# A fused attention and soft-mixture kernel: fewer key columns in the loads, one small input carried in another's rows, and the first output columns stored in pairs of tiles

## The chip, the cores and the metric

The kernel runs on one core of a Trainium2 chip, as one launch. The metric is the device time of an execution in microseconds, the median of three runs. The times in the profile and in the rows below are microseconds from the start of the span of one profiled execution, if not marked ns.

## What is computed

Two blocks follow each other. The first is chunked attention: 4 batches x 8 heads, 768 tokens, head size 64. A chunk of 32 queries sees 8 memory keys, 16 tokens to its left, its own 32 and 8 to its right. The second is a soft mixture of 8 experts with 4 slots each; its input `x` is the attention's output as 3072 rows of 512.

```python
for c in range(24):                       # chunks of 32 tokens, per batch and head
    k_full = concat(mem_k, k[max(0, 32*c - 16) : min(768, 32*c + 40)])
    a = softmax(q[chunk c] @ k_full.T / 8);  out[chunk c] = a @ v_full
x = out as (3072, 512)
logits = x @ phi                          # phi: 512 x 32 slots
d = softmax over the rows of logits;  slot_input = d.T @ x          # 32 x 512
slot_out = relu(slot_input[e] @ w1[e]) @ w2[e]   # w1[e]: 512 x 1024, w2[e]: 1024 x 512
return softmax over the slots of logits @ slot_out
```

## The kernel before

Everything is float32, and every instruction is kept in the order in which the program writes it (`InOrder`, lines 52 to 64), so each engine's queue is what the text below says. All transfers are issued by SP, in one queue over 16 DMA engines, and a transfer uses all 16.

**Attention.** The 3072 rows are cut into 12 units of 256 (three to a batch; lines 20 to 36). Unit U needs queries (512 KB, `load_qk`, line 214), keys (two transfers, for even and odd heads, `load_k`, line 198) and values (768 KB, `load_v`, line 219). A unit's keys stand as a stream of 312 columns for each of four head pairs: memory keys, then two chunks, and so on, with 16 columns ahead and 8 behind. Where the unit before in the same batch holds the first 24 columns already (units 2, 4, 5, 7, 8, 10 and 11, `has_head`, line 67), only 288 are loaded and POOL copies the 24 over (`head_from_last`, `head_from_own`, lines 203 to 212). In a batch's first unit the first 16 columns, and in its last unit the last 8, are zeros that belong to no token; their scores are overwritten with -1e30 before the softmax (lines 265 to 267). Values come in three slabs of 512 columns; POOL builds a fourth slab and moves rows (`place_v`, line 223, five copies).

The loop at line 456 runs over the units as a pipeline: normalize unit U-1, transpose its output and unit U's weights, scores and softmax of U+1, values of U; then SP gets the loads of U+3 and a share of the weights (`load_w`). After every second unit 512 rows go through the logits and the dispatch sums (lines 327 to 419). `phi` is read first in `part_logits` (line 327), in unit 2; its load is issued once, at line 451, behind the values of unit 2.

**Experts.** Weights are kept in slabs of 128 x 1024, in places that come free one after the other (lines 140 to 154), mostly loaded two slabs to a transfer of 1 MB with rows of 8 KB. `w1` is used in `expert_in` (line 614), `w2` in `expert_out` (line 663). The output's 512 columns are worked in two halves (`NBLK` = 2, 256 columns each): for a half, eight experts are summed in one accumulation, the sum is copied (`slot_copy`, line 674), summed over its four groups by a matmul and copied again (`slot_rows`, line 677). Then six tiles of 512 rows (`combine`, line 689) each take four matmuls, copies by DVE and ACT into a free slab (`stage`, line 687) and a store of 512 KB with rows of 4 KB (line 710).

The order at the end is written out by hand (lines 713 to 727). While TensorE works the second half's experts 1 to 5, the first half's tiles 0 to 4 are combined, one behind each expert; the sixth comes behind the second half's sums, and then the six tiles of the second half:

```python
    shls, among = [None] * NBLK, (1, 2, 3, 4, 5)
    ...
    late = [(0, G) for G in range(len(among), NG)] + [(1, G) for G in range(NG)]
    for i, (blk, G) in enumerate(late):
        combine(blk, G, shls[blk], i % 2 == 1)
        if i == 0:
            shls[1] = slot_rows(1)
```

With the last argument true, `combine` takes four single PSUM banks and DVE makes two copies; with false it takes a pair of banks, and DVE makes one wide copy. Tile names in the rows: `s` scores, `a` values' sums, `kh` the copied key columns, `so` the experts' sums, `r` the sum over groups, `D` its copy for the second half, `o` a tile's matmuls.

## Time and profile before

| | |
|---|---|
| median of 3 runs | 160.84 us (160.62 to 160.93) |
| profiled execution | 159.95 us, of which the span is 158.2 us |
| TensorE, DVE, ACT, POOL busy | 141.4, 98.9, 74.4, 58.8 us |
| moved by DMA | 63.34 MB, 12457 packets, mean 400 GB/s |
| read from and written to HBM | 56.67 and 6.29 MB |

In the profile a group's line gives engine, operation, what it writes and reads, and how often; a transfer's landing is counted from its issue by SP until all 16 DMA engines have reported. The DMA share is the mean over the 16 engines; packets overlap a little, so that it can stand above 1.

### The profile page before, as it was taken

The page shows a single profiled execution, that of the slowest core. Times are in us where ns is not written, and L with a number is a line of the kernel's source. Part 1 is how long each engine was busy: PE and PEld are TensorE (multiplying, and loading weights), DVE is VectorE, ACT ScalarE, POOL GpSimd, SP SyncE. Part 2 cuts the span into 40 slices and gives each one's busy share as a digit, 9 for nine tenths or more (in the row PEclk, how much of TensorE's full clock was granted, in tenths as well). Part 3 has the DMA queues.
Part 4 walks back from the last instruction along what each step waited for, and adds up shares of the span by engine and source line. Part 5 has one row for each costly group of instructions (what it writes and reads, how often), then busy time and mean ns, then how long its engine had stood idle before and what let it go on. Part 6 is the DMA issues. An engine that isn't in the chain of part 4 may idle for free.

```text
span 158.2 us, 5938 instructions
## 1 busy us (share of the span) xinstructions
PE 141.4 (89%) x2577; PEld 99.5 (63%) x2577; DVE 98.9 (63%) x195; ACT 74.4 (47%) x165; POOL 58.8 (37%) x87
## 2 busy tenths in 40 slices
PE   7998789999999697999997998999999999998900
PEld 3457669786878594868785867656655555444500
DVE  7098969889787777698889489644552101334810
ACT  3032484866659466676585658140232200334710
POOL 8329858766083947655519450400000000000000
PEclk9999999999999999999999999999999999999995
DMA  5999999999999999999999999999999999999995
GB/s 158 327 410 420 408 420 423 421 412 428 410 431 410 421 421 423 415 429 410 423 419 424 433 419 421 419 402 339 407 425 421 431 421 427 414 418 369 374 410 207
DMA packets 12457, 63.34 MB, mean 400 GB/s; under 512 B 1552, under 2 KB 1680, under 8 KB 8848
## 3 DMA queue, kind: packets, MB, share of 16 engines
q1 hardware_dynamic: 12432, 62.97, 97.5%
q8 instruction: 20, 0.33, 0.8%
q14 instruction: 5, 0.04, 0.1%
HBM read 56.67 MB, written 6.29 MB: 398 GB/s over the span
## 4 chain that ended last, share of the span: by engine, by line
PE 79%; DVE 7%; issue 4%; DMA 3%; ACT 3%; POOL 1%; DVEq 0%; POOLq 0%
PE a L62 14%; PE s L62 12%; PE so L62 9%; PE h L62 9%; PE pt_ps L62 7%; PE xt_ps L62 6%; PE o L62 5%; PE D_ps L62 4%; PE lp L62 3%; DMA k<-in_kT_dram 3%; PE l L62 2%; DVE pt L62 2%; PE fill L62 2%; PE ht_ps L62 2%; DVE z L62 1%
## 5 line engine op out<-in xcount | busy, mean ns | idle before, releaser
L62 POOL COPY v<-v 32x512 f32<-32x512 f32 (+1 forms) x60 | 46.8, 780 | 29.0 <-DMA v<-in_vw_dram 25.5
L62 PEld LDWEIGHTS a<-v,pt 128*64 128x64 f32 x768 | 24.3, 138 | 13.8 <-ACT pt L62 6.6
L62 PE MATMUL a<-v,pt 128*64 128x64 f32 x768 | 27.0, 225 | 4.1 <-issue 2.5
L62 ACT COPY pt<-pt_ps 64x512 f32<-64x512 f32 (+1 forms) x48 | 26.1, 544 | 0.9
L62 PE MATMUL s<-k,q 128*32 128x128 f32 x712 | 24.4, 275 | 0.5 <-issue 0.3
L62 ACT ACTIVATE p<-p 128x512 f32<-128x512 f32 x24 | 15.1, 631 | 16.6 <-DVE p L62 16.2
L62 PEld LDWEIGHTS s<-k,q 128*32 128x32 f32 x712 | 20.7, 110 | 3.4 <-issue 3.3
L62 DVE TENSOR_REDUCE mx<-s 128x8 f32<-128x512 f32 x24 | 16.5, 688 | 6.5 <-PE s L62 6.2
L62 ACT COPY xT<-xt_ps 128x512 f32<-128x512 f32 x22 | 12.8, 586 | 12.6 <-PE xt_ps L62 12.5
L62 DVE TENSOR_TENSOR p<-s,mx 128x512 f32<-128x512 f32 x24 | 16.6, 692 | 0.8
L62 PE MATMUL pt_ps<-ident,p 128*128 128x128 f32 x96 | 15.0, 279 | 1.3 <-issue 1.1
L62 DVE TENSOR_TENSOR x<-a,z 128x512 f32<-128x512 f32 x22 | 14.7, 682 | 1.4 <-PE a L62 1.4
L62 DVE TENSOR_REDUCE z<-p 128x16 f32<-128x1040 f32 (+1 forms) x13 | 14.9, 1143 | 0.0
L62 PE MATMUL xt_ps<-ident,x 128*128 128x128 f32 x88 | 13.1, 273 | 0.6 <-DVE x L62 0.6
L62 PEld LDWEIGHTS pt_ps<-ident,p 128*128 128x128 f32 x96 | 10.7, 141 | 4.0 <-issue 2.8
L62 PE MATMUL h<-w,siT 128*32 128x256 f32 x208 | 12.1, 381 | 0.0
L62 PE MATMUL so<-w,pt 128*32 128x256 f32 x176 | 10.9, 382 | 0.0
L62 PEld LDWEIGHTS xt_ps<-ident,x 128*128 128x128 f32 x88 | 10.1, 141 | 0.9 <-DVE x L62 0.8
L62 PE MATMUL fill<-lp 128*128 128x512 f32 x12 | 8.5, 849 | 1.1 <-DVE lp L62 1.1
L62 PEld LDWEIGHTS h<-w,siT 128*32 128x32 f32 x208 | 6.4, 110 | 4.2 <-issue 0.3
L62 PEld LDWEIGHTS so<-w,pt 128*32 128x32 f32 x176 | 5.1, 109 | 4.7 <-issue 2.0
L62 ACT ACTIVATE xT<-h,rzd 128x512 f32<-128x512 f32 x4 | 2.8, 688 | 11.1 <-PE h L62 11.1
(119 smaller groups left out, 159.0 us busy)
## 6 DMA issues: line engine op xcount, KB each, us to landing
w<-in_w_dram SPq DMA_DIRECT2D x23, 1024.0 KB, 11.4
v<-in_vw_dram SPq DMA_DIRECT2D x12, 768.0 KB, 9.8
q<-in_qT_dram SPq DMA_DIRECT2D x12, 512.0 KB, 8.5
k<-in_kT_dram SPq DMA_DIRECT2D x14, 288.0 KB, 8.8
k<-in_kT_dram SPq DMA_DIRECT2D x10, 312.0 KB, 8.5
k<-in_w_dram SPq DMA_DIRECT2D x2, 1024.0 KB, 12.7
v<-in_w_dram SPq DMA_DIRECT2D x2, 1024.0 KB, 13.4
out_dram<-w SPq DMA_DIRECT2D x4, 512.0 KB, 6.4
```

Of the source, the lines that this page charges most:

```text
L62: return self.tc.keep_in_program_order(f(*args, **kwargs))
```

## The change

There are three edits.

Keys: a batch's first unit no longer loads the 16 columns of no token and a batch's last unit no longer loads its 8 (`k_cut`). The first unit's rows land 16 columns further on in the buffer, and the score matmul of the chunk at the edge reads what stands beside them, old but finite numbers; their scores are overwritten as before.

phi: the array `phi` is gone as an input of its own; its 64 KB stand behind the values of unit 1 in the same rows, `load_v(1)` brings them into the fourth slab's place, and POOL copies them out before it builds that slab.

Stores: tiles 0 and 1, 2 and 3, 4 and 5 of the first half are stored by one transfer each, 1 MB with rows of 8 KB, when the second of the two is copied. The sixth tile moves behind expert 6 of the second half, so that the second half's sums are followed at once by `slot_rows(1)` and its six tiles. These are stored one by one, as before.

```diff
+def k_cut(U):
+    t = U % UPB
+    return (LEFT if t == 0 else HALO if has_head(U) else 0), (RIGHT if t == UPB - 1 else 0)
...
-    def k_shift(U):
-        return HALO if has_head(U) else 0
+    def k_row(U):
+        lo, hi = k_cut(U)
+        return (LEFT if U % UPB == 0 else 0), KW - lo - hi
...
     def load_k(U, pars=range(2)):
-        n = NPAIR * (KW - k_shift(U))
+        at, n = k_row(U)
         for par in pars:
-            sp.dma_start(k_buf[U % 2][par:P:2, par, 0:n], kT[U, par, :, 0:n])
+            sp.dma_start(k_buf[U % 2][par:P:2, par, at:at + NPAIR * n], kT[U, par, :, 0:NPAIR * n])
...
     def load_v(U):
         if U < NU:
-            sp.dma_start(v_buf[U % NV][:, 0:3, :], vw[U].rearrange("p (s n) -> p s n", n=DM))
+            n = 3 * DM + (NKC * NSLOT if U == 1 else 0)
+            sp.dma_start(v_buf[U % NV].rearrange("p s n -> p (s n)")[:, 0:n], vw[U, :, 0:n])
...
         v = v_buf[U % NV]
+        if U == 1:
+            pool.tensor_copy(out=phi_sb.rearrange("p c s -> p (c s)"), in_=v[:, 3, 0:NKC * NSLOT])
...
-    sp.dma_start(phi_sb.rearrange("p c s -> p (c s)"), phi)
...
+    out_pair = out[0].rearrange("g p u n -> (g p u n)").rearrange("(h p m) -> h p m", h=NG // 2, p=P)
...
+    def store(blk, G):
+        if blk:
+            sp.dma_start(out[blk, G], stage[NG * blk + G])
+        elif G % 2:
+            f, o = places[order[G - 1]]
+            sp.dma_start(out_pair[G // 2], f[:, o:o + 2 * PIECE])
...
-        sp.dma_start(out[blk, G], o_sb)
+        store(blk, G)
...
-    shls, among = [None] * NBLK, (1, 2, 3, 4, 5)
+    shls, among = [None] * NBLK, (1, 2, 3, 4, 5, 6)
...
-    late = [(0, G) for G in range(len(among), NG)] + [(1, G) for G in range(NG)]
-    for i, (blk, G) in enumerate(late):
-        combine(blk, G, shls[blk], i % 2 == 1)
-        if i == 0:
-            shls[1] = slot_rows(1)
+    shls[1] = slot_rows(1)
+    for G in range(NG):
+        combine(1, G, shls[1], G % 2 == 1)
```

The rows of all values in HBM become 512 B longer, of which only unit 1's carry anything and only unit 1's are loaded in full. The host puts the paired rows of the first half back in order.

## Rows read from the trace of the kernel before

**Rows 1.** The page: busy tenths of the DMA engines in 40 equal slices of the span, the rate in each slice, and the share of the DMA engines' time that SP's queue took.
```profile
DMA  5999999999999999999999999999999999999995
GB/s 158 327 410 420 408 420 423 421 412 428 410 431 410 421 421 423 415 429 410 423 419 424 433 419 421 419 402 339 407 425 421 431 421 427 414 418 369 374 410 207
q1 hardware_dynamic: 12432, 62.97, 97.5%
```

**Rows 2.** Four transfers by themselves: the last weight load, the first store, the first store of the second half, the last store. Of the first and the last the issue on SP (start, duration); those of the other two stand in rows 3. Behind each issue its time to landing; the landings are in the order of the four.
```profile
125.21 0.33 SPq L62 DMA_DIRECT2D w<-in_w_dram  x1
...
DMA to landing us min/median/max: 17.0/17.0/17.0
...
DMA to landing us min/median/max: 7.0/7.0/7.0
...
DMA to landing us min/median/max: 3.5/3.5/3.5
...
151.74 1.15 SPq L62 DMA_DIRECT2D out_dram<-q  x1
...
DMA to landing us min/median/max: 5.5/5.5/5.5
```

**Rows 3.** Instructions in order of time: start, time from the first start to the last end of the group, engine and what it is. First around the first store, then around the end of the experts.
```profile
135.01 0.71 PE L62 MATMUL o<-v 32*128 32x256 f32 x8
...
135.66 1.07 PE L62 MATMUL so<-w,pt 128*32 128x256 f32 x16
...
136.52 1.99 SPq L62 DMA_DIRECT2D out_dram<-w  x2
...
136.66 0.71 PE L62 MATMUL o<-v 32*128 32x256 f32 x8
...
142.24 1.93 PE L62 MATMUL so<-w,pt 128*32 128x256 f32 x32
...
144.10 0.71 PE L62 MATMUL o<-v 32*128 32x256 f32 x8
144.24 0.42 DVE L62 COPY v<-so 128x256 f32<-128x256 f32 x1 [1.21 <-PE so L62]
...
144.74 0.70 PE L62 MATMUL r<-v,gsum 128*128 128x256 f32 x2
...
145.48 0.37 ACT L62 COPY D<-r 128x256 f32<-128x256 f32 x1
...
145.91 4.35 PE L62 MATMUL o<-D,v 32*128 32x256 f32 x48 [0.46 <-ACT D L62]
...
147.46 0.93 SPq L62 DMA_DIRECT2D out_dram<-v  x2
```

**Rows 4.** Busy time by stretch, from 126 us on. Columns: stretch, its length, then busy us of PE, PEld, DVE, ACT and POOL with the number of instructions, the granted clock, the DMA share and GB/s.
```profile
126.00:136.00 10.00, 10.00 (x174) 5.51 (x170) 0.66 (x2) 0.57 (x2) 0.00 (x0) 1.00 1.01 427
...
144.00:150.00 6.00, 5.47 (x62) 3.36 (x58) 4.34 (x10) 3.94 (x13) 0.00 (x0) 1.00 0.89 358
150.00:156.00 6.00, 0.25 (x8) 0.00 (x0) 0.84 (x2) 0.77 (x3) 0.00 (x0) 0.82 1.02 410
```

**Rows 5.** Busy time by quarters of a microsecond behind the issue at 147.46; columns as in rows 4.
```profile
147.75:148.00 0.25, 0.25 (x7) 0.00 (x0) 0.25 (x2) 0.17 (x1) 0.00 (x0) 1.00 0.53 213
148.00:148.25 0.25, 0.25 (x7) 0.21 (x8) 0.25 (x2) 0.03 (x1) 0.00 (x0) 1.00 0.32 131
148.25:148.50 0.25, 0.25 (x8) 0.23 (x5) 0.25 (x2) 0.25 (x2) 0.00 (x0) 1.00 1.08 442
```

**Rows 6.** What TensorE waited for between 5 and 100 us: us in total, times, the longest. Only two of the ten answers are shown, the largest and the one for a transfer.
```profile
PE a L62 <- issue: 2.5, 2, 1.4
...
PE s L62 <- DMA k<-in_kT_dram: 0.2, 1, 0.2
```

**Rows 7.** Transfers again: all key loads by size (number, KB each, median landing), and by themselves the values of unit 1, and the issues of the values of unit 2 and of phi with the landing of each, in this order.
```profile
k<-in_kT_dram SPq DMA_DIRECT2D x14, 288.0 KB, 8.8
k<-in_kT_dram SPq DMA_DIRECT2D x10, 312.0 KB, 8.5
...
L62 SPq DMA_DIRECT2D v<-in_vw_dram x1: 585/585/585, 5.4 to 5.4; - x1
...
DMA to landing us min/median/max: 8.7/8.7/8.7
...
10.78 0.33 SPq L62 DMA_DIRECT2D v<-in_vw_dram  x1
11.53 0.33 SPq L62 DMA_DIRECT2D phi<-in_phi_dram  x1
...
DMA to landing us min/median/max: 11.0/11.0/11.0
...
DMA to landing us min/median/max: 10.4/10.4/10.4
```

**Rows 8.** POOL and TensorE in order of time between 14 and 24 us: the 24 key columns of unit 2 in two parts, the values of unit 1, and the values' sums of unit 1. In brackets the engine's idle time before it and what ended it.
```profile
14.98 0.34 POOL L62 COPY kh<-k 128x192 f32<-128x192 f32 x1
...
15.39 4.09 POOL L62 COPY v<-v 32x512 f32<-32x512 f32 x5
...
19.96 0.45 POOL L62 COPY kh<-k 128x320 f32<-128x320 f32 x1 [0.49 <-DMA k<-in_kT_dram]
...
23.09 1.09 PE L62 MATMUL a<-v,pt 128*64 128x64 f32 x30 [0.30 <-ACT pt L62]
```

## The prediction

> **What bounds the kernel now.** I read the page first: TensorE is busy 141.4 of 158.2 us, but the 16 DMA engines are busy in every slice from the second to the last but one, at some 400 to 430 GB/s, and SP's queue alone fills 97.5% of their time [rows 1]. So there are two candidates, and the chain of waits alone does not choose between them: it goes back along TensorE and stops at the last copy, before the last stores have landed.

> Next came the landings of single transfers [rows 2]. The last weight load, issued at 125.2, lands 17.0 us later, at 142.2; the first store, issued at 136.52 [rows 3], lands 7.0 us later, at 143.5, right behind it. The twelfth and last store lands at 151.74 + 5.5 = 157.24. Eleven stores in 157.24 − 143.5 = 13.7 us are 1.25 us each, with no hole, although the shares of the engines show holes between 144 and 150 (0.89, [rows 4]). So some engine always had work, and the end is the end of the DMA queue: **whatever leaves the queue before the tail should bring the end forward, as long as the stores are issued in time.**

> How much time do they have? The shortest landing is that of the first store of the second columns, issued at 147.46: 3.5 us, at 150.96 [rows 2, 3]. It found the queue nearly empty: in the half microsecond from 147.75 the engines were busy 0.53 and 0.32 of the time, and full again from 148.25 [rows 5]. TensorE itself waits for almost no transfer after its first scores (0.2 us for k; its large stalls are unexplained "issue", 2.5 us in one group, [rows 6]), so a faster queue does not make it faster. It reaches the tail when its own work is done.

> **The change, part by part, on the queue.** (1) Keys. Four units lose 16 columns and four lose 8: (4 x 16 + 4 x 8) x 4 pairs x 4 B x 128 rows = 196,608 B. At the 427 GB/s of 126 to 136 us [rows 4] that is 0.46 us. The transfers stay 24 in number [rows 7]; only their rows shorten. Score matmuls still take 64 columns each, so no compute changes.

> (2) phi. The 64 KB travel in the second value load. phi was issued at 11.53 and landed 10.4 later, at 21.93; the value load before it landed at 21.78 [rows 7]. So it cost 0.15 us in the queue, give or take 0.1 of rounding, and 64 KB at 427 GB/s are 0.15. Gain: 0 to 0.1, taken as 0.05. The second values, 64 KB longer, land up to 0.15 later; POOL takes them up only at 15.39, though issued at 5.4 and 8.7 us later, at 14.1, they were there [rows 7, 8], and the keys and values queued before phi's old place shift by at most 0.1. The new POOL copy of 128x128 is nearest to its 128x192 copy of 0.34 us; behind it POOL idles 0.49 us for keys before 19.96 [rows 8], which covers it. If that cover were gone, the scores of the third unit would start 0.3 us late, and behind them TensorE waits 0.30 for ACT's copies of the transposed weights, until 23.09, anyway [rows 8]. Cost: nothing. SP saves one issue, which nobody waits for.

> (3) Stores by 8 KB rows. No store of that kind is in the trace. Weight loads by 8 KB rows ran at 427 GB/s, stores by 4 KB rows at 410 [rows 4]: 1 MB in 2.46 against 2.56 us, so 0.30 for three pairs; by the landings, 2.46 against 2 x 1.25, 0.13. A store may also gain nothing. I take 0.2, between 0 and 0.3. A pair starts only when its second tile is copied, but the first pair (about 138.2, when the second store went) still stands behind weights that land until 142.2, and so do the others behind it.

> Sum on the queue: 0.46 + 0.05 + 0.2 = 0.7 us (0.46 to 0.86). **Alone it would end the queue at 156.5.**

> **The change on TensorE.** The sixth tile of the first columns moves ahead of the last expert. A tile's matmuls take 0.65 us of TensorE's order there (135.01 to 135.66), an expert's 1.00 (135.66 to 136.66), two experts in a row 1.86 (142.24 to 144.10) [rows 3]. Now the last two are parted: 1.00 + 0.65 + 1.00 = 2.65 in place of 1.86, so the last expert ends 0.79 later. Behind it stands a chain that keeps its length: copy of the sums (DVE 144.24), matmul r (144.74), copy to D (ACT 145.48), first matmuls of the second columns (145.91). In the kernel before, the sixth tile ran beside that DVE copy and cost TensorE nothing; that cover is given up. The first tile of the second columns now takes the path with one wide DVE copy, 1.51 us from matmul to store (135.01 to 136.52) against 1.55 (145.91 to 147.46). Its store is issued at 147.46 + 0.79 − 0.04 = 148.21. The first keys are 5% shorter, and the first scores wait for them [rows 6]: −0.05. So about **148.15, which is 0.7 later than before, in a queue that is 0.7 shorter.** [...]

> Before this store the queue would be through: three pairs of 2.46 after weights that land at 142.2 − 0.5 = 141.7 end at 149.1. How long does a store take that finds idle engines? From below: the engines fill again 0.8 to 1.0 us after the issue at 147.46 [rows 5], then 512 KB at 410 GB/s are 1.28, together 2.3, with some 0.2 until the last engine's end is seen: 2.5. From above: 3.5, the shortest landing, which still has a rest of the queue in it. I take 2.5, since that row shows engines at work (0.32) just before. Then 148.15 + 2.5 = 150.65 for the first store, against 149.1 + 1.25 = 150.35 if the queue decided. Five more at 1.25 to 1.28 give 156.9 to 157.05, against 157.24: **0.2 to 0.35 earlier; I take 0.27.**

> [...]

> **How it stands to the runs.** The profiled execution took 159.95 us (span 158.2); the median of the runs is 160.84. I take the difference off the median: 160.84 − 0.27 = 160.57. The 0.9 us between them lies on a part that no row shows, and rivals differ by where it lies. A measurement here tells 0.2% (0.32 us) from no change.

> **Rivals.**
> - *The queue decides to the end.* If the 0.9 us of the timed runs is a slower queue, the store issued at 148.15 still finds work ahead of it, and the whole 0.7 arrives: 160.15 (159.95 to 160.4). For it: the even 1.25 us of all landings, and a margin of only 0.3 us (150.65 against 150.35). Against: the same margin, since the profile has it on the other side.
> - *The last chain decides, at a higher price.* A store into idle engines takes 3.5 us, as the only nearly empty case in the trace did [rows 2]: 148.15 + 3.5 + 6.25 = 157.9, slower by 0.66, 161.5; 3.0 us, half way to the forecast's 2.5, give 161.0. It decides as soon as such a store takes over 157.24 − 6.25 − 148.15 = 2.84 us. Against: the queue was not empty in that row, so 3.5 is too much. [...]
> - *Nothing to be seen.* Stores by 8 KB rows run as slowly as by 4 KB and the restart costs 0.2 more: the two shifts cancel, 160.8.

> **How the numbers follow.** Forecast 0.45: its 0.2 to 0.35 straddles the bound, so 0.18 faster, 0.26 the same, 0.01 slower. Queue to the end 0.27: 0.26 faster, 0.01 the same. Last chain dearer 0.18: 0.15 slower, 0.03 the same. Nothing to be seen 0.10: 0.08 the same, 0.02 slower. Sums: faster 0.44, same 0.38, slower 0.18. The range reaches from the upper bound of the queue's gain (160.84 − 0.86 = 160.0) to the half-way case of the dear chain with a little over it, 161.2; the forecast's own is 160.4 to 160.75.

> **What the profile after would show.** HBM reads 0.2 MB less; no phi transfer; three stores of 1 MB, landing 2.4 to 2.5 us apart, the first at about 144.1; the first store of the second columns issued at 148.1 to 148.2 with a landing of 2.4 to 2.7 us; a deeper hole in the DMA's share just before it; the last store issued with the queue about one store shorter. The forecast is wrong if that store is issued before 147.9 or lands over 3 us after its issue, if weights land no earlier than 142.0, or if TensorE's stalls of about 1 us ("issue") change in number.

## Result and profile after

Six runs of the changed kernel have a median of 163.17 us (161.68 to 165.88), six of the kernel before beside them 160.8 us (160.5 to 161.7). The ratio is **1.0104 (95%: 1.0059 to 1.015)**: slower by about 1%, 1.7 us, where 0.2% were forecast as a gain. Executions of every version scatter by some us, and a ratio leaves out those that took over 1.5% longer than the version's fastest, among them the profiled ones of the change, e1, e4, e5 and e9. The profiled execution took 164.72 us (span 162.9), 3.9 us more than the median before; so it shows more loss than the ratio does.

The page, as in [rows 1], with TensorE's granted clock and the queue of instructions:

```profile
PEclk9999999699999999999999999999999999999985
DMA  5999999989999999999999999999999999998795
GB/s 157 339 376 420 411 428 412 424 331 322 396 373 366 394 422 411 421 421 389 389 403 430 423 424 422 422 404 366 360 426 420 428 424 428 412 394 356 314 404 235
q1 hardware_dynamic: 11856, 62.77, 96.2%
q8 instruction: 20, 0.33, 0.8%
```

The 0.2 MB are gone (62.77 for 62.97 MB). But there is a new hole in the rate near 33 to 41 us (331 and 322 GB/s) and a deeper one near the end (314). SP issues loads when TensorE's work lets it, so a queue that runs short at 33 us tells of a TensorE that was late before.

**The tail**, as in [rows 3]; then single stores with the time from issue to landing, as in [rows 2]: the three pairs (issued at 142.62, 145.9 and 149.19), the first store of the second half (152.62) and the last (156.9).

```profile
146.69 1.07 PE L62 MATMUL so<-w,pt 128*32 128x256 f32 x16
...
147.69 0.71 PE L62 MATMUL o<-v 32*128 32x256 f32 x8
...
148.33 1.07 PE L62 MATMUL so<-w,pt 128*32 128x256 f32 x16
...
149.47 0.42 DVE L62 COPY v<-so 128x256 f32<-128x256 f32 x1 [0.34 <-PE so L62]
149.95 0.70 PE L62 MATMUL r<-v,gsum 128*128 128x256 f32 x2 [0.55 <-DVE v L62]
150.69 0.37 ACT L62 COPY D<-r 128x256 f32<-128x256 f32 x1 [1.56 <-PE r L62]
151.11 1.15 PE L62 MATMUL o<-D,v 32*128 32x256 f32 x16 [0.46 <-ACT D L62]
...
152.62 0.99 SPq L62 DMA_DIRECT2D out_dram<-v  x2
```

```profile
out_dram<-w SPq DMA_DIRECT2D x1, 1024.0 KB, 5.6
...
out_dram<-w SPq DMA_DIRECT2D x1, 1024.0 KB, 6.2
...
out_dram<-k SPq DMA_DIRECT2D x1, 1024.0 KB, 5.4
...
out_dram<-v SPq DMA_DIRECT2D x1, 512.0 KB, 3.2
...
out_dram<-q SPq DMA_DIRECT2D x1, 512.0 KB, 5.0
```

The first store of the second half comes at 152.62, 5.2 us later than in [rows 3], and lands 3.2 us after its issue; the third pair landed at 149.19 + 5.4 = 154.6, when this store was already issued. The five behind it end 6.1 us later, at 161.9. The trace has the report of each of the 16 DMA engines: 15 had done the third pair by 153.06, the last at 154.55, and from there its reports come 1.2 us apart to the end (155.78, 157.00, 158.22, 159.44, 160.69, 161.92). In the half microsecond around that issue little more than one engine's share (1/16 is 0.06) is busy:

```profile
152.50:153.00 0.50, 0.39 (x8) 0.38 (x9) 0.50 (x3) 0.50 (x3) 0.00 (x0) 1.00 0.09 33
```

So the end is the queue of one engine, which always had work. Of the 5.2 us the new order explains 0.7 (below). The rest came from far ahead.

**The early stage.** TensorE between 20 and 36 us, first before, then after:

```profile
20.47 0.30 PE L62 MATMUL s<-kh,q 128*32 128x128 f32 x1 [0.35 <-POOL kh L62]
...
23.09 1.97 PE L62 MATMUL a<-v,pt 128*64 128x64 f32 x60 [0.30 <-ACT pt L62]
24.99 0.66 PE L62 MATMUL pt_ps<-ident,p 128*128 128x128 f32 x4
...
26.88 1.95 PE L62 MATMUL s<-k,q 128*32 128x128 f32 x64
```

```profile
21.04 0.30 PE L62 MATMUL s<-kh,q 128*32 128x128 f32 x1 [1.10 <-POOL kh L62]
...
23.02 1.84 PE L62 MATMUL a<-v,pt 128*64 128x64 f32 x54
27.52 0.66 PE L62 MATMUL a<-v,pt 128*64 128x64 f32 x10 [2.66 <-issue]
28.11 1.12 PE L62 MATMUL pt_ps<-ident,p 128*128 128x128 f32 x4
...
31.52 1.95 PE L62 MATMUL s<-k,q 128*32 128x128 f32 x64
```

The third unit's scores wait 1.10 us for the copied keys in place of 0.35, and then TensorE stands 2.66 us within one group of matmuls, waiting for nothing that the trace names. The wait for the keys costs little: when the value sums run, at 23.0, TensorE is about 0.1 us behind, since the kernel before waits 0.30 there for ACT. The scores of unit 3 start at 31.52 in place of 26.88: 4.6 us lost, of which the stall is 2.66. The next fence has POOL between 14 and 24 us, as in [rows 8], and then the busy time by stretch (columns as in [rows 4]).

```profile
15.36 0.34 POOL L62 COPY kh<-k 128x192 f32<-128x192 f32 x1
15.65 0.28 POOL L62 COPY phi<-v 128x128 f32<-128x128 f32 x1
15.99 4.08 POOL L62 COPY v<-v 32x512 f32<-32x512 f32 x5
20.54 0.45 POOL L62 COPY kh<-k 128x320 f32<-128x320 f32 x1 [0.47 <-DMA k<-in_kT_dram]
```

```profile
24.00:28.00 4.00, 1.34 (x38) 1.20 (x34) 1.90 (x3) 0.98 (x2) 3.46 (x6) 0.98 1.01 415
28.00:32.00 4.00, 4.00 (x37) 3.72 (x39) 2.09 (x3) 0.96 (x2) 3.15 (x4) 0.59 1.05 426
32.00:36.00 4.00, 4.00 (x114) 3.05 (x105) 3.17 (x6) 3.37 (x7) 2.55 (x5) 1.00 0.88 334
...
144.00:150.00 6.00, 5.45 (x85) 2.25 (x73) 2.70 (x5) 2.13 (x7) 0.00 (x0) 1.00 0.85 352
```

phi's copy takes 0.28 us, as priced, and POOL still waits 0.47 for the keys behind it: its cover holds. TensorE is busy a third of the time from 24 to 28. Behind that stall its granted clock is 0.59 of full speed as a mean of four us (0.50 from 28 to 31 us); the next four transposes take 1.12 us instead of 0.66, and from their start to the scores of unit 3 it takes 3.41 us instead of 1.89: 1.5 of the 4.6 us.

### The profile page after: what moved, and what is told of

Read it like the earlier page. It is cut to its first block, busy times and chain, and to the rows that moved or that the text cites. A ratio compares the mean times of both kernels' runs of the same rounds, so it can differ in the third digit from the quotient of the medians.

```text
span 162.9 us, 5930 instructions
## 1 busy us (share of the span) xinstructions
PE 141.3 (87%) x2577; PEld 100.8 (62%) x2577; DVE 99.1 (61%) x195; ACT 74.4 (46%) x165; POOL 58.8 (36%) x88
## 3 DMA queue, kind: packets, MB, share of 16 engines
q1 hardware_dynamic: 11856, 62.77, 96.2%
## 4 chain that ended last, share of the span: by engine, by line
PE 70%; DMA 9%; DVE 8%; issue 6%; POOL 1%; ACT 1%; SPq 0%; DVEq 0%; POOLq 0%
PE s L62 12%; PE a L62 12%; DMA k<-in_kT_dram 9%; PE so L62 9%; PE h L62 9%; PE pt_ps L62 6%; PE xt_ps L62 5%; PE o L62 4%; PE D_ps L62 3%; PE lp L62 2%; PE l L62 2%; DVE mx L62 2%; PE ht_ps L62 1%; DVE p L62 1%; DVE z L62 1%
## 5 line engine op out<-in xcount | busy, mean ns | idle before, releaser
L62 PEld LDWEIGHTS a<-v,pt 128*64 128x64 f32 x768 | 24.9, 138 | 15.6 <-issue 7.3
L62 PE MATMUL a<-v,pt 128*64 128x64 f32 x768 | 27.8, 225 | 6.2 <-issue 4.8
L62 PE MATMUL s<-k,q 128*32 128x128 f32 x712 | 23.4, 274 | 1.8 <-DMA k<-in_kT_dram 1.8
L62 PE MATMUL pt_ps<-ident,p 128*128 128x128 f32 x96 | 16.0, 292 | 0.9 <-issue 0.9
L62 PE MATMUL xt_ps<-ident,x 128*128 128x128 f32 x88 | 13.9, 285 | 0.5 <-DVE x L62 0.4
L62 PEld LDWEIGHTS pt_ps<-ident,p 128*128 128x128 f32 x96 | 11.4, 147 | 3.6 <-issue 2.7
L62 PEld LDWEIGHTS xt_ps<-ident,x 128*128 128x128 f32 x88 | 10.9, 149 | 0.9 <-DVE x L62 0.9
L62 PE MATMUL s<-kh,q 128*32 128x128 f32 x56 | 7.4, 276 | 1.1 <-POOL kh L62 1.1
L62 PE MATMUL fill<-lp 128*128 128x512 f32 x12 | 7.3, 740 | 1.1 <-DVE lp L62 1.1
L62 PE MATMUL D_ps<-x,dT 128*32 128x512 f32 (+1 forms) x56 | 7.3, 507 | 0.9 <-issue 0.8
## 6 DMA issues: line engine op xcount, KB each, us to landing
w<-in_w_dram SPq DMA_DIRECT2D x23, 1024.0 KB, 10.4
```

The lines of the kernel that those rows point to most:

```text
L62: return self.tc.keep_in_program_order(f(*args, **kwargs))
```

## Experiments

All ratios are to runs of the kernel before on the same chip in the same hour. The theories behind the expectations came as the traces did: first which of the three edits costs, then where phi's bytes stand, then what holds TensorE.

**The change again, and its parts alone.** e1 is the whole change once more; e2 cuts only the keys; e3 only moves phi; e4 has only the stores in pairs and the new order at the end.

```diff
e1  (the whole change)
e2  + k_cut, k_row, k_window;  phi and tail as before
e3  + n = 3 * DM + (NKC * NSLOT if U == 1 else 0);  - sp.dma_start(phi_sb..., phi)
e4  + store(blk, G), among = (1, 2, 3, 4, 5, 6), slot_rows(1) ahead of the six tiles
```

> The changed kernel once more, for the spread of its executions and a second profile. Theory 1 (the early stage): in the profile after, TensorE stands still from 24.87 to 27.52 in the value sums of unit 1, where an instruction fetch that went at 21.51 in the kernel before goes at 24.92, then runs at half the clock for some 3 us; all later work is 4.5 us late. It expects a ratio of 1.010 to 1.02, a wide spread, and in the profile an idle time of TensorE of at least 1 us between 20 and 45 us that the kernel before does not have. Theory 2 (the tail): the last chain is 0.8 us later and the queue has no margin left; it expects 161.0 to 161.6, a narrow spread, and an experts' stage that starts within 0.3 us of the kernel before (125.5).

> Only the key columns are cut; phi by itself and the stores as before. Theory 1: if the shorter keys are what shifts the early stage, 161.5 to 163 (ratio 1.005 to 1.015) with a new stall of TensorE before 45 us; if not, 160.3 to 160.5 (0.46 us less in the queue). Theory 2: 160.35, ratio 0.997, since the tail is untouched and the queue decides it.

> Only phi is moved into the values of unit 1; keys and stores as before. Theory 1: if the 64 KB ahead of the keys of unit 2 shift the early stage, 161.5 to 163 with a new stall of TensorE before 45 us; if not, 160.7 to 160.8. Theory 2: 160.75, no difference that can be told.

> Only the first half's stores by pairs and the new order of the last tiles; keys and phi as before. Theory 1: nothing early changes, so the experts' stage starts where it did and the time is within 0.3 us of the kernel before. Theory 2: the whole loss is here: the first store of the second half is issued at about 148.2 instead of 147.46 and the time is 161.0 to 161.6. By the prediction on record: the queue is only 0.2 shorter and the last chain 0.75 later, so 160.8 to 160.9.

Measured: e1 1.0114 (1.0025 to 1.0204), e2 1.007 (1.0023 to 1.0117), e3 1.0073 (1.0029 to 1.0116), e4 1.001 (0.9959 to 1.006). The change costs 1% again. phi's move alone costs most of it, the tail little. e3's trace does not have the new stall that the expectation tied to its loss. Keys alone also came out slower, but the kernel before against itself (e5) differs by half as much, and with phi in another place (e11) all the cut keys cost less; what e2 lost stays open.

**The floor of the comparison, the order alone, the change without its tail, phi one unit later.**

```diff
e5  (the kernel before)
e6  + among = (1, 2, 3, 4, 5, 6), slot_rows(1) ahead of the six tiles;  single stores
e7  the change with the old tail
e8  + n = 3 * DM + (NKC * NSLOT if U == 2 else 0)   # only this: phi behind unit 2's values
```

> The kernel before, unchanged, measured as an edit would be, for how far two equal kernels differ here and for a second profile of it. The four runs so far say that TensorE reaches the experts at 107.6 in the profile of before and at 109.7 to 112.1 in all five later ones, even in e4_stores, whose early stage is unchanged. Theory 1 (keys and phi shift the early stage): ratio 1.000 with the experts at 107 to 108.5. Theory 3 (the profile of before was an early execution, and the early stage moves by some us from one execution to the next whatever the kernel): experts at 108.5 to 112 here too, and from their start to the first store of the second half 39.85 us, from that store to the last landing 9.2 to 9.5 instead of 9.76.

> Only the order of the last tiles: the sixth tile of the first half behind expert 6, all stores single. Theory 2 (the last chain sets the end, the queue has no say): from the experts' start to the first store of the second half 40.55 us instead of 39.85, the last landing 9.3 to 9.5 behind that store, so 0.5 to 0.8 us slower than the kernel before (ratio 1.003 to 1.005). The prediction on record, by its forecast: the queue decides unless the store finds it empty, so the loss is 0 to 0.3.

> The change without its tail: keys cut and phi in the values' rows, stores and order as before. Theory 2: 0.7 less than the whole change, so a ratio to before of about 1.005 if the early stage costs what keys and phi alone showed (1.007 each), and 1.000 or below if these were the early stage's own scatter. Theory 1: the two losses add, 1.010 to 1.015, the whole of the change's loss. In the profile the tail is that of before: 39.85 us from the experts' start to the first store of the second half.

> phi in the values of unit 2 instead of unit 1, so that its 64 KB stand behind the keys of unit 2 in the queue and not ahead of them; all else as before. Theory 1 (the 64 KB ahead of the keys of unit 2 make the scores of unit 2 late): the loss of e3_phi (ratio 1.007) goes, 0.998 to 1.002. Theory 3 (scatter): no difference to e3_phi that can be told, both within 0.5% of before.

Measured: e5 1.0034 (0.998 to 1.0088), e6 1.0036 (0.9983 to 1.0089), e7 1.0106 (1.002 to 1.0192), e8 **0.9989 (0.9942 to 1.0037)**. A comparison here tells about half a per cent. The loss is there without the new tail, and it is gone when the same 64 KB stand behind the values of unit 2, that is behind the keys of unit 2 in the queue instead of ahead of them.

**The place of the bytes, by itself.** e9 and e10 move phi with 256 KB in place of 64 (three quarters of it unused) behind unit 1's or unit 2's values; e11 is the whole change with phi in unit 2's values; e12 is e11 with the old tail and the keys cut from unit 3 on only.

```diff
e9   + n = 3 * DM + (DM if U == 1 else 0)
e10  + n = 3 * DM + (DM if U == 2 else 0)
e11  - if U == 1:   + if U == 2:          (in load_v and place_v of the change)
e12  e11 with k_cut only where U > 2, and the old tail
```

> The kernel e3_phi with the row behind the values of unit 1 lengthened from 128 to 512 columns (the other 384 carry zeros that nothing reads): 256 KB instead of 64 KB ahead of the queries and keys of unit 2, 0.6 us of the queue at 427 GB/s, 192 KB more in the whole. Theory 1 (what stands ahead of the keys of unit 2 sets TensorE back): 0.8 to 2 us slower than e10_wide_unit2, which moves the same bytes; keys of unit 2 land 0.5 us later than in e3_phi against the first keys. Theory 3 (scatter): within 0.3 us of e10_wide_unit2; both 0 to 0.5 us slower than the kernel before for the longer queue.

> The kernel e8_phi_later with the same 512 columns behind the values of unit 2: the same bytes as e9_wide_unit1, but behind the keys of unit 2. Theory 1: ratio to the kernel before 0.998 to 1.003, as e8_phi_later plus at most 0.46 us for 192 KB where the queue decides. Theory 3: as e9_wide_unit1.

> The whole change, but with phi behind the values of unit 2. Theory 1, if phi's place is the main part of the early loss: the time falls by 0.7 to 1.2 us against the whole change (ratio to before 1.002 to 1.006, what is left being the tail's 0.3 to 0.7 us). If the keys carry as much (e2_keys showed 1.007): 1.006 to 1.010. Theory 2: no difference to the whole change, 1.010.

> phi behind the values of unit 2, the key columns cut only from unit 3 on (so that the loads of units 0 to 2 are those of the kernel before, but for phi's place), stores and order of the kernel before. Theory 1: nothing early is set back and the tail is the old one, so 0.2 to 0.8 us faster than the kernel before (ratio 0.995 to 0.999). Theory 3: no difference that can be told, 0.998 to 1.002.

Measured: e9 1.0102 (1.0048 to 1.0155), e10 1.0048 (1.0007 to 1.0089), e11 1.0044 (1.0015 to 1.0074), e12 1.0033 (1.0 to 1.0066). In all three pairs that differ in phi's place alone the early place is dearer: e3 to e8 by 0.8%, e1 to e11 by 0.7%, e9 to e10 by 0.5% (one pair alone would not be enough, since the intervals overlap, and only e9 and e10 ran side by side). With four times the bytes the early place costs no more, so it is not the bytes' time in the queue. The single executions up to e12 say the same: of 36 with phi behind unit 1's values one was below 161.3 us, of 47 with phi behind unit 2's 25, of 92 of the kernel before 54. But this count scatters too: of the 48 of e2, e4, e5 and e6, which leave phi alone, 12 were, and of e5, the kernel before, 3 of 12. None of these versions beats the kernel before; e10 and e12 were forecast at 0.998 to 1.003 and 0.995 to 0.999 and came out slower.

**What holds TensorE.** The traces of all versions have the stall of about 2 us at the same matmul or not at all: in the change, e1, e2, e4, e5 and e9 TensorE stops with ten matmuls of unit 1's value sums left. The kernel before can have it too (e5, the same program). The queue of instructions in the profile has 20 transfers of 16 KB, for some 5,220 TensorE instructions, so one to 261, and the stalls lie 256 TensorE instructions apart, or a multiple of that. A block is counted here as the 256 from one such place to the next; block 3 begins with the 706th instruction, at which the stall after the change ends (27.52). The table counts every TensorE instruction in order of time and is worked out from the traces; a fetch is one packet of that queue, and that it brings the block behind the one during which it starts is my reading of the table.

```
                                     before  e5     after  e8     e11    f1     f3
block 2 entered (450th instruction)  18.97   19.07  18.79  19.58  20.34  19.20  18.46
second fetch starts                  21.51   24.27  24.92  21.79  22.90  22.56  22.18
wait of the fetch                     2.54    5.20   6.13   2.21   2.56   3.36   3.71
stall before block 3                  none    1.9    2.7    none   none   none   none
first expert matmul                  107.61  111.07 112.06 107.73 108.50 103.68 108.43
```

In all traces TensorE enters a block 2.2 us or more after its fetch has started; so a fetch that starts late holds TensorE, by my reading. In the 17 profiled executions with full weights (f1 is the one without) the seven with a stall before block 3 are those whose second fetch waited over 5 us, and they took 162.5 to 164.7 us; the ten others took 160.0 to 162.2. The last four experiments test whether the late fetches are the reason.

```diff
f1  - return min(NW, W_FIRST + int(W_PER_UNIT * units))   + return W_FIRST      # on the kernel before
f2  - dummies(3, fill)                                                            # on the kernel before
    + for n in range(0, 3 * 512, 128):
    +     pe.matmul(fill[:, n % 512:n % 512 + 128], lhsT=warm, rhs=warm, start=True, stop=True)
f3  the same on the change
f4  - load_w(W_FIRST)     # ahead of the loop, on the change
```

> The kernel before with all weight loads but the first MB held back until unit 9 (w_target returns W_FIRST); nothing is left out, 12 MB come later, so the end comes late whatever the theory (170 to 185 us). The question is the attention stage. In the kernel before TensorE stands still at the same places about 1.0 to 1.6 us long (53.6, 61.3, 85.8 in its trace), 256 TensorE instructions (16 KB of program) apart or a multiple of that; the profiler's instruction queue shows a 16 KB fetch that starts 3.4 to 3.8 us after TensorE enters one such block, and TensorE enters the next 2.4 to 2.5 us after that start. Theory A (the fetch waits on the DMA engines behind queued loads): with engines that idle between the units' loads the fetch starts under 2.5 us after the block is entered, the three long stalls vanish or fall under 0.5 us, and the values' sums of unit 8 are over at least 3 us earlier than in the kernel before, counted from the first scores. Theory B (the stalls belong to the places in the program, whatever the queue holds): the same stalls of 1.0 to 1.6 us, and that stretch within 0.7 us of before.

f1: the expert matmuls start at 103.68, 96.6 us after the first scores, against 100.9 before; unit 8's value sums end 67.95 us after the first scores against 71.91, 4.0 earlier. All that TensorE waits for as "issue" between 5 and 108 us, first before, then f1, each followed by two halves of the stage (last two columns: DMA share and GB/s):

```profile
55.20 0.34 PE L62 MATMUL a<-v,pt 128*64 128x64 f32 x4 [1.38 <-issue]
62.64 1.15 PE L62 MATMUL a<-v,pt 128*64 128x64 f32 x30 [1.09 <-issue]
74.88 0.74 PE L62 MATMUL s<-k,q 128*32 128x128 f32 x18 [0.29 <-issue]
87.12 0.49 PE L62 MATMUL pt_ps<-ident,p 128*128 128x128 f32 x3 [1.07 <-issue]
```

```profile
28.00:56.00 28.00, 26.52 (x583) 20.88 (x575) 23.48 (x41) 18.47 (x38) 16.76 (x25) 1.00 1.02 419
56.00:84.00 28.00, 26.62 (x570) 21.12 (x569) 22.51 (x39) 19.23 (x41) 14.89 (x22) 1.00 1.02 420
```

```profile
83.20 0.49 PE L62 MATMUL pt_ps<-ident,p 128*128 128x128 f32 x3 [0.67 <-issue]
```

```profile
28.00:56.00 28.00, 27.90 (x622) 22.74 (x615) 24.70 (x43) 19.66 (x40) 20.52 (x30) 1.00 0.80 279
56.00:84.00 28.00, 27.25 (x618) 22.10 (x608) 24.51 (x42) 19.50 (x41) 15.96 (x25) 1.00 0.83 297
```

With the engines busy 0.80 instead of 1.02 of the time the stalls are gone, and the same 28 us hold 39 and 48 more matmuls. The fetches of this stage start 0.3 to 2.5 us after their block is entered (with one of 2.9 at its begin), not 3.2 to 3.8 (one of 4.9) as before. Where the weights come, the stall is back, at the same instruction (83.20 here, 87.12 before). So these stalls are the queue's doing, not the program's. f1 is one execution (177.24 us as a whole, since its weights end late), and it says nothing of the stall before block 3: up to 19 us its loads are those of the kernel before.

> The kernel before with its first three warm-up matmuls of 512 columns cut into twelve of 128: the same work, 36 TensorE instructions more, so that every later boundary of 256 instructions lies 36 instructions earlier in the program. Theory A (TensorE is held by the fetch of its next 256 instructions, about 6.1 us from block to block): the stalls move 36 instructions up, and by the durations between the boundaries their sum falls from 5.5 to 4.65 us; ratio 0.994 (0.988 to 1.000). Theory B (the stalls belong to the places in the program): the same instructions stall, ratio 0.999 to 1.003.

> The whole change with the same cut of the warm-up (36 TensorE instructions more ahead of the first scores). Theory A: the long stall in the values' sums of unit 1 (2.66 us at 24.87 in the profile of the change) ends 18 matmuls earlier in these sums or is shorter, and the kernel gains as the kernel before does: ratio 1.000 to 1.008 (the whole change alone had 1.010 and 1.011). Theory B: 1.009 to 1.014, the stall at the same instruction.

f2 took 1.0008 (0.9968 to 1.0048), f3 **1.0018 (0.9971 to 1.0065)**. In f2's trace the stall in unit 1's value sums stands with 28 matmuls left, 18 earlier than in the change:

```profile
18.72 0.56 PE L62 MATMUL a<-v,pt 128*64 128x64 f32 x11 [1.63 <-issue]
26.50 1.03 PE L62 MATMUL a<-v,pt 128*64 128x64 f32 x28 [1.21 <-issue]
```

36 instructions, 18 of them matmuls, moved it by just these. In time the kernel before gained nothing (the 0.6% by adding up durations was wrong: a new stall of 1.63 us came at 18.72, where the first fetch was late). The whole change went from 1.010 and 1.011 to 1.002 without a byte, a transfer or a result of it altered; but they did not run side by side, and the intervals overlap a little (the change's from 1.0059, f3's to 1.0065). f3's trace has no stall before block 3, but it has the new one, 1.73 us, at 18.46.

> The whole change without the early load of the first MB of weights (the line load_w(W_FIRST) ahead of the loop; that MB comes with unit 0's share, behind the keys of unit 3). Theory C (the loss is that unit 2's keys and values land later, 20.39 in place of 19.82 for the keys): they land 2.4 us earlier, at about 18, the scores of unit 2 no longer wait, ratio 1.000 to 1.005. Theory A (the loss is the second instruction fetch, which waits behind a long queue of loads): as many bytes stand in the queue at 19 us, the fetch starts 5 us or more after its block is entered, and the ratio stays at 1.007 to 1.014.

f4 took 1.0045 (0.9991 to 1.0099): by its middle within theory C's forecast, but the interval holds much of theory A's as well. Unit 2's keys land at 18.09, as theory C had it; the second fetch waits 3.55 us, not the 5 of theory A, and there is no stall before block 3; the third waits 5.12 and TensorE stalls 1.12 one block later. The time doesn't tell the two apart.

## Why the prediction was wrong

**The step that failed** is "a faster queue does not make TensorE faster. It reaches the tail when its own work is done", and with it "Cost: nothing" for phi's place. The rows for it were there: the largest wait of TensorE was 2.5 us of "issue" [rows 6], which I called unexplained and then left alone. f1 shows that these stalls hang on the queue (with the engines at 0.80 the stage to unit 8's value sums is 4.0 us shorter), and e3 to e12 that phi's place ahead of unit 2's keys costs 0.5 to 0.8%, that is 0.8 to 1.3 of the 1.7 us; the tail is another 0.3 (below). The prediction named "if TensorE's stalls of about 1 us ("issue") change in number" as what would prove it wrong; between 5 and 100 us the waits for "issue" in value sums went from 2.5 us to 4.8:

```profile
PE a L62 <- issue: 4.8, 3, 2.7
PE s L62 <- DMA k<-in_kT_dram: 1.8, 2, 1.3
PE s L62 <- POOL kh L62: 1.1, 1, 1.1
```

Whether phi's place costs its time by making the second fetch late is not shown. The stall before block 3 stands in three of the five traces with phi early (after, e1, e9; not in e3 and e7) and in three of the nine others up to e12 (e2, e4, e5), so it comes without phi's move too, and it costs an execution more than the 1.7 us of the ratio. Unit 2's keys land 0.6 us later (20.39 for 19.82) and the scores wait 0.7 longer, which is less than the loss; the second fetch waits 1.7 to 3.7 us in some traces and 5.1 to 6.8 in others, and no view shows why. In e3 and e7 the first scores came late (8.2 and 8.1 us) and ran at a lower granted clock (from 8 to 10 us 0.50 and 0.62 as a mean), in 3.39 and 3.33 us; they came as late in e11 (8.2), with phi behind unit 2's values, at a clock of 1.00 and in 1.95 us. In e3:

```profile
8.22 3.39 PE L62 MATMUL s<-k,q 128*32 128x128 f32 x64 [2.68 <-DMA k<-in_kT_dram]
```

**"Whatever leaves the queue before the tail should bring the end forward"** is the other step that failed. The kernel before ends as the prediction read it: the last engine reports the last weights at 142.25 and then twelve stores some 1.25 us apart. It is so after the change too, but for the second pair (below), and the queue still decides; but its last weights land at 145.67 instead of 142.2 - 0.5. They follow TensorE: in the 17 profiled executions with full weights they land 33.6 to 35.2 us behind the first expert matmul, and SP issues the last twelve of these loads from 1.13 us behind that matmul on, before and after:

```profile
108.74 16.80 SPq L62 DMA_DIRECT2D w<-in_w_dram  x12
...
113.19 15.79 SPq L62 DMA_DIRECT2D w<-in_w_dram  x12
```

That matmul comes at 107.61 in the profiled execution before, the earliest of all these, and at 107.73 to 112.06 in the others; against these 4.5 us the 0.5 us of keys and phi are not to be seen, and neither e2 nor e12, which load fewer keys ahead of an unchanged tail, gained (1.007, 1.0033). That the loads' tie to TensorE is the reason is read from the traces; no edit tested it. The 0.9 us between the profiled execution and the median "lies on a part that no row shows", and one execution cannot tell more; in the second trace of the same program (e5, 163.14 us) the first expert matmul comes 3.5 us later. And a forecast of 0.2% was beyond what a comparison tells here: the kernel before against itself came out at 1.0034.

**The order of the tail** was right: from the first expert matmul to the issue of the second half's first store it is 39.84 to 39.86 us with the old order and 40.54 to 40.56 with the new, 0.70 more, as worked out (148.15 against 147.46).

**The store into idle engines** takes 2.5 us, as forecast: 15 of the 16 engines reported the first store of the second half 2.46 to 2.62 us after its issue, and in e6 all 16 did after 2.45 to 2.65. The 3.16 us until it had landed are not that price. The last engine had the third pair until 154.55 and needed 1.23 us more. So "Before this store the queue would be through" failed for one engine, and of the rivals the one in which the queue decides to the end had the bound right, though not the time; the last chain at a higher price did not come true. The 0.2 us that the forecast adds until the last engine's end is seen stood in no row; here these 15 reports lie 0.16 us apart, in e6 all 16 some 0.2. From the first expert matmul to the last landing the new tail takes 49.65 to 50.04 us (seven traces, mean 49.9), the old 49.1 to 50.2 (ten, mean 49.6): about 0.3 us lost in place of 0.27 won.

**The bytes** were right (0.2 MB less, no phi transfer), and the first pair landed 2.5 us behind the last weights, the third 2.4 behind the second, as worked out. But these weights landed at 145.7, not 141.7, and the second pair 3.9 us behind the first (issued at 145.9, landed at 152.1). TensorE's lateness is not the reason, since the issue is the same for all 16 engines: 15 had done this pair by 150.62, and one took 1.5 us longer. e4 has the same (3.85 us), e1 and e11 do not (2.4); what holds that engine stays open. By the third pair (2.44 us against two stores of 1.25) rows of 8 KB gain some 0.06 us a pair, 0.2 in all, as forecast.

## What to carry over

A stall of an engine that the profile puts on nothing is a term of the sum, not noise: look how many instructions lie between two of them, and whether the instruction queue's transfers stand ahead of them. On this core the fetch of TensorE's program waits for the loads too (3.2 to 3.8 us at a DMA share of 1.02, 0.3 to 2.5 at 0.80), and moving a small early transfer cost more than its bytes (0.8 to 1.3 us by three pairs of runs; 64 KB at 427 GB/s are 0.15 us, the 256 KB of the least dear pair 0.6). Before an end is put on one of two bounds, see more than one execution, and look at the reports of the single DMA engines: a mean share of 0.09 can hide the one that still has work and sets the end.

## What the runs showed of the hardware

The end of a transfer is the end of its slowest engine, and the 16 lie far apart: 0.2 us for the store above in e6, 2.6 us for the second pair after the change, some 3 us for the first store before the change.

An even cut of the warm-up matmuls, 36 instructions more and nothing else, came with 0.9% less time for the changed kernel and none for the kernel before: where the blocks of a program end is a parameter of such a kernel, and its effect is not to be had by adding up stalls.
